# A new hand-written order and another layout of the attention weights in a one-core hash-attention and feed-forward kernel

## The chip, the core and the metric

One core of a Trainium2 chip runs the kernel. The core has TensorE (PE, the matrix unit), VectorE (DVE), ScalarE (ACT), GpSimd (POOL), SyncE (SP, which here only issues transfers) and 16 DMA engines. Every engine takes its own instructions strictly in the order in which they were written; semaphores tie the engines together. Matrix products land in PSUM, an accumulator memory of eight banks of 512 float32 for each of 128 partitions; everything else lives in SBUF.

The metric is the device time of one execution in microseconds (us); a median of several runs is given. The profile comes from one execution.

## The reference

Four batches, eight heads, 768 positions, head size 64; the model width is 512 and the hidden width 2048. Six sign bits of a projection give each query and key a bucket, and only keys of the query's own bucket are attended to. What follows is a layer norm, a two-layer feed-forward with a ReLU, and a residual.

```
q_bits = (einsum('bhsd,dk->bhsk', q, proj) > 0); k_bits likewise
q_bucket = sum(q_bits * powers); k_bucket likewise
mask = q_bucket[:, :, :, None] == k_bucket[:, :, None, :]
scores = where(mask, (q @ k.T) / sqrt(D), -1e9)
attn = softmax(scores) ; x = (attn @ v) laid out as (B, S, 512)
xn = (x - mean) / sqrt(var + 1e-6) * g_ln
out = x + relu(xn @ w_ch1) @ w_ch2
```

## The kernel before

The work is cut into twelve *units*: unit u is batch u // 3 and 256 of its 768 queries. A unit has six *steps*: two groups of four heads (g) times three blocks of 256 keys. Step s belongs to unit s // 6, so steps 0 to 17 are batch 0 and steps 18 to 71 are batches 1 to 3.

The kernel has no loops over this work. The string `ORDER` (lines 17 to 115) lists some 1,120 words such as `S.t.19.2`: an operation, the engine it is issued on (t TensorE, v VectorE, a ScalarE, p GpSimd, s SyncE) and its arguments. The last lines of the kernel body walk through the string and call one short function for each word. So the order of the words is the program order of every engine, of SP's and POOL's transfers too. The words that matter:

- `lx`, `tn`, `ca`, `ha`, `bi` (batch 0) and `LX`, `tu`, `CA`, `hm`, `bt`, `mo` (later batches): load queries and keys, transpose them (DVE, line 247), cast them to bf16, form the bucket bits (a small float32 product, then a comparison). `mo` is a DMA of 4.5 KB that puts one piece of the bits into place; there are 16 for each batch and group, 96 in all, on SP (line 421).
- `S` (line 444): 24 matmuls that make the scores of one step, 128 keys by 256 queries, twice, for four heads. The bucket bits enter as a further product, so that keys of another bucket come out far below zero.
- `E` (line 454): `exp` on ScalarE, PSUM to SBUF, 128 x 1024 elements, two instructions for each step (heads 0 and 1, heads 2 and 3): 144 in all.
- `A` (line 463): 16 matmuls for each step that multiply the exponentials with the values and a column of ones, into the two PSUM banks `acc`.
- `na`, `nb`, `nc`, `ce` (lines 474 to 489): DVE divides by the sum and makes the layer norm's statistics; `fl` (line 498) transposes the normalised rows by DMA, issued on SP.
- `F` (line 516): 8 matmuls for 256 of the hidden columns; `R` (line 524 on ScalarE, line 526 on VectorE): ReLU. Eight pairs for each unit, through one PSUM bank, `f1`.
- `D` (line 532): the second feed-forward product, 16 matmuls of 512 columns for each half of a unit, written as four quarters, into the bank `f2`. `Z` (line 541) adds the residual and `O` (line 545 on) stores.

PSUM is full: `scA` and `scB` (two banks each) for scores, `acc` (two), `f1` and `f2`. Before `acc` is first needed, the steps 0 to 5 rotate over three pairs, by the table `SC_PAIRS` at line 151.

The transposes work on 32 x 32 blocks, so a column of the scores stands for a query in a permuted order. Units 0 to 2 keep that order: the attention result comes out with permuted rows, and a unit is stored by four DMAs of 32 partitions and 128 KB each (`out_view`). From unit 3 on (`U_TURNED = 3`, line 163) `E` writes its output turned, each element four places from the one before it, so that rows come out in the order of the output tensor, and a unit is stored by one DMA of 128 partitions and 512 KB (`out_turned`, line 555). The last unit is stored in six pieces of 64 partitions (line 558).

Of the kernel before, what the change touches and what calls it, by code (L numbers as in the profile page):

```python
# [17 lines left out]
mem.v on.p.1 on.p.0 lp.a pf.v lx.s.0.1.1.3 tn.v.0.1.2 ca.p.0.1.2 tn.v.0.1.1 lx.s.0.0.0.1 tn.v.0.0.0 ca.a.0.0.0  # L18
ca.a.0.1.1 lx.s.1.0.0.1 warm.t ha.t.0.1.2 bi.v.0.1.2 tn.v.1.0.0 ca.p.1.0.0 ha.t.0.0.0 bi.v.0.0.0 lx.s.0.1.0.1
tn.v.0.1.0 ca.a.0.1.0 ha.t.1.0.0 bi.v.1.0.0 pmem.p p32.p S.t.2.2 E.a.2.1 E.a.2.0 lv.s.0.0.4 cv.p.0.0.2 ha.t.0.1.1  # L20
bi.v.0.1.1 ha.t.0.1.0 lx.s.1.1.0.3 tn.v.1.1.2 ca.p.1.1.2 S.t.1.2 E.a.1.1 E.a.1.0 lx.s.1.0.1.3 ha.t.1.1.2 bi.v.0.1.0
S.t.0.2 E.a.0.0 E.a.0.1 lg.s tn.v.1.1.1 ha.t.1.1.1 ca.p.1.1.1 bi.v.1.1.2 S.t.5.2 E.a.5.1 tn.v.1.1.0 ca.p.1.1.0
ha.t.1.1.0 cv.p.0.0.0 A.t.1.2 A.t.0.2 bi.v.1.1.1 lw1.p.0 E.a.5.0 S.t.4.2 E.a.4.1 lw1.p.1 lx.s.0.0.1.3 tn.v.0.0.2
tn.v.0.0.1 ha.t.0.0.1 ca.v.0.0.1 lw2.p.1 E.a.4.0 bi.v.1.1.0 sv.t.0 LX.s.1.0.1 tu.v.1.0.1.3 tu.v.1.0.1.1 tu.v.1.0.1.2
lw1.p.3 tu.v.1.0.1.0 lw2.p.0 CA.p.1.0.1.1 tn.v.1.0.2 A.t.2.2 bi.v.0.0.1 S.t.6.2 E.a.6.0 E.a.6.1 ha.t.1.0.2 sw.v.0
na.v.0.0 nb.v.0.0 S.t.3.2 nc.v.0.0 E.a.3.1 bi.v.1.0.2 ha.t.0.0.2 lv.s.0.4.4 cv.p.0.4.0 cv.p.0.4.2 sv.t.4 LX.s.1.0.0
tu.v.1.0.0.0 tu.v.1.0.0.2 lv.s.1.4.1 S.t.8.2 E.a.3.0 A.t.3.2 E.a.8.0 A.t.5.2 E.a.8.1 A.t.4.2 ca.v.1.0.2 tn.v.1.0.1
ca.v.1.0.1 bi.v.0.0.2 ha.t.1.0.1 S.t.7.2 E.a.7.1 E.a.7.0 LX.s.1.1.1 lw1.p.2 sw.v.4 na.v.0.1 nb.v.0.1 A.t.8.2
nc.v.0.1 A.t.6.2 ce.v.0.0 bi.v.1.0.1 ft.t.0.0 fc.a.0.0 S.t.10.2 E.a.10.0 E.a.10.1 ce.v.0.1 ft.t.0.1 rs.p.0
tu.v.1.0.0.1 A.t.7.2 fc.v.0.1 F.t.0.0 R.a.0.0 CA.v.1.0.0.0 LX.s.1.1.0 S.t.11.2 E.a.11.1 E.a.11.0 lw2.p.2  # L30
tu.v.1.0.0.3 CA.a.1.0.0.1 hm.t.1.0 bt.v.1.0 mo.s.1.0.3.0 mo.s.1.0.0.0 mo.s.1.0.2.3 mo.s.1.0.0.3 mo.s.1.0.1.2
mo.s.1.0.0.1 mo.s.1.0.1.3 mo.s.1.0.3.3 mo.s.1.0.0.2 F.t.0.7 R.v.0.7 lw2.p.3 S.t.9.2 E.a.9.1 CA.p.1.0.1.0 F.t.0.6
F.t.0.3 na.v.1.0 nb.v.1.0 A.t.10.2 ca.v.0.0.2 E.a.9.0 S.t.14.2 E.a.14.1 tu.v.1.1.0.3 A.t.9.2 R.v.0.6 mo.s.1.0.2.2
E.a.14.0 nc.v.1.0 R.v.0.3 lv.s.1.0.0 A.t.11.2 na.v.1.1 F.t.0.4 R.a.0.4 LX.s.2.1.1 F.t.0.1 R.a.0.1 S.t.13.2 E.a.13.0
E.a.13.1 nb.v.1.1 A.t.14.2 nc.v.1.1 ce.v.1.0 ce.v.1.1 fl.s.1.1 fl.s.1.0 F.t.0.5 R.a.0.5 tu.v.1.1.0.0 lv.s.1.4.2
F.t.0.2 R.a.0.2 LX.s.2.0.0 lv.s.1.4.3 lv.s.1.0.3 tu.v.1.1.0.1 mo.s.1.0.1.1 mo.s.1.0.1.0 mo.s.1.0.2.1 tu.v.1.1.1.3
S.t.12.2 E.a.12.1 E.a.12.0 tu.v.1.1.1.0 tu.v.1.1.0.2 CA.a.1.1.0.1 mo.s.1.0.2.0 lv.s.1.0.1 mo.s.1.0.3.1 LX.s.2.0.1
D.t.0.0.0 D.t.0.0.1 D.t.0.0.2 D.t.0.0.3 S.t.16.2 E.a.16.0 E.a.16.1 mo.s.1.0.3.2 tu.v.1.1.1.1 F.t.1.7 R.v.1.7
A.t.13.2 A.t.12.2 na.v.2.0 F.t.1.2 R.a.1.2 S.t.17.2 E.a.17.1 E.a.17.0 tu.v.1.1.1.2 CA.p.1.1.1.1 hm.t.1.1 Z.v.0.0
D.t.0.1.0 bt.v.1.1 mo.s.1.1.3.2 mo.s.1.1.3.0 mo.s.1.1.2.1 mo.s.1.1.1.1 mo.s.1.1.0.1 mo.s.1.1.0.0 mo.s.1.1.1.2  # L40
mo.s.1.1.3.1 F.t.1.0 R.a.1.0 S.t.15.2 E.a.15.0 E.a.15.1 rs.p.1 nb.v.2.0 nc.v.2.0 A.t.16.2 A.t.17.2 mo.s.1.1.0.3
CA.v.1.1.0.0 tu.v.2.0.1.2 tu.v.2.0.1.1 LX.s.2.1.0 F.t.1.6 R.a.1.6 D.t.0.1.1 CA.p.1.1.1.0 tu.v.2.0.0.0 mo.s.1.1.1.0
mo.s.1.1.0.2 lv.s.1.0.2 cv.p.1.0.0 A.t.15.2 na.v.2.1 nb.v.2.1 nc.v.2.1 ce.v.2.0 fl.s.2.0 ce.v.2.1 rs.p.2 on.p.2
F.t.1.5 R.a.1.5 S.t.19.2 E.a.19.0 F.t.1.3 R.a.1.3 tu.v.2.0.1.3 CA.p.2.0.1.1 mo.s.1.1.3.3 mo.s.1.1.1.3 E.a.19.1
fl.s.2.1 D.t.0.1.2 D.t.0.1.3 Z.v.0.1 O.s.0.3 tu.v.2.0.0.1 F.t.1.1 R.a.1.1 sa.p.1.0.1 S.t.20.2 tu.v.2.0.0.3
mo.s.1.1.2.0 tu.v.2.0.0.2 CA.v.2.0.0.1 tu.v.2.0.1.0 E.a.20.1 F.t.1.4 R.a.1.4 lv.s.1.4.0 cv.p.1.4.0 D.t.1.0.0
D.t.1.0.1 D.t.1.0.2 D.t.1.0.3 Z.v.1.0 E.a.20.0 S.t.18.2 E.a.18.0 mo.s.1.1.2.2 E.a.18.1 F.t.2.2 R.v.2.2 D.t.1.1.0
F.t.2.4 R.a.2.4 mo.s.1.1.2.3 S.t.22.2 E.a.22.0 F.t.2.1 R.v.2.1 cv.p.1.0.2 A.t.18.2 A.t.19.2 sa.p.1.0.0 sb.p.1.0
sa.p.1.0.2 lv.s.3.4.0 lv.s.3.4.2 lv.s.3.4.1 F.t.2.0 R.v.2.0 E.a.22.1 S.t.21.2 E.a.21.1 lv.s.3.4.3 su.p.1.0
sa.p.1.4.2 sa.p.1.4.1 sa.p.1.4.0 sb.p.1.4 E.a.21.0 A.t.20.2 sp.t.1.0 sc.v.1.0 na.v.3.0 nb.v.3.0 nc.v.3.0 D.t.1.1.1  # L50
F.t.2.5 R.v.2.5 S.t.23.2 E.a.23.0 E.a.23.1 D.t.1.1.2 D.t.1.1.3 O.s.0.0 F.t.2.7 CA.a.2.0.1.0 S.t.24.2 E.a.24.1
E.a.24.0 su.p.1.4 cv.p.1.4.2 lv.s.2.0.3 lv.s.2.0.1 lv.s.2.0.2 A.t.22.2 R.v.2.7 sp.t.1.4 Z.v.1.1 O.s.1.3 O.s.1.2
O.s.1.0 A.t.23.2 A.t.21.2 sc.v.1.4 F.t.2.3 R.a.2.3 S.t.25.2 E.a.25.1 E.a.25.0 D.t.2.0.0 na.v.3.1 nb.v.3.1 nc.v.3.1
ce.v.3.0 fl.s.3.0 O.s.0.1 ce.v.3.1 rs.p.3 fl.s.3.1 CA.a.2.0.0.0 O.s.0.2 hm.t.2.0 tu.v.2.1.1.0 bt.v.2.0 mo.s.2.0.3.2
mo.s.2.0.3.1 mo.s.2.0.2.2 mo.s.2.0.1.0 mo.s.2.0.1.2 mo.s.2.0.0.0 tu.v.2.1.0.3 tu.v.2.1.1.2 mo.s.2.0.2.3 LX.s.3.0.0
S.t.26.2 E.a.26.0 E.a.26.1 mo.s.2.0.2.0 LX.s.3.1.0 tu.v.2.1.0.2 CA.v.2.1.0.1 mo.s.2.0.1.1 mo.s.2.0.0.2 D.t.2.0.1
D.t.2.0.2 F.t.2.6 R.a.2.6 tu.v.2.1.1.3 lv.s.2.0.0 mo.s.2.0.3.0 mo.s.2.0.2.1 S.t.28.2 E.a.28.1 E.a.28.0 A.t.26.2
F.t.3.7 R.v.3.7 A.t.24.2 D.t.2.0.3 Z.v.2.0 mo.s.2.0.1.3 S.t.29.2 E.a.29.0 E.a.29.1 O.s.1.1 mo.s.2.0.0.3 A.t.25.2
na.v.4.0 D.t.2.1.0 tu.v.2.1.1.1 LX.s.3.0.1 F.t.3.1 R.a.3.1 S.t.27.2 E.a.27.0 E.a.27.1 D.t.2.1.1 D.t.2.1.2
mo.s.2.0.3.3 sa.p.2.0.0 F.t.3.4 R.a.3.4 S.t.31.2 E.a.31.1 E.a.31.0 tu.v.2.1.0.1 F.t.3.0 R.a.3.0 nb.v.4.0 A.t.29.2  # L60
A.t.27.2 A.t.28.2 na.v.4.1 S.t.32.2 E.a.32.0 E.a.32.1 F.t.3.5 R.v.3.5 CA.p.2.1.1.1 CA.p.2.1.1.0 D.t.2.1.3 Z.v.2.1
O.s.2.2 F.t.3.3 R.a.3.3 S.t.30.2 E.a.30.1 F.t.3.2 R.a.3.2 nc.v.4.0 D.t.3.0.0 E.a.30.0 nb.v.4.1 A.t.32.2 F.t.3.6
nc.v.4.1 ce.v.4.1 fl.s.4.1 R.a.3.6 ce.v.4.0 fl.s.4.0 S.t.34.2 E.a.34.1 E.a.34.0 A.t.30.2 O.s.2.0 mo.s.2.0.0.1
cv.p.2.0.2 tu.v.2.1.0.0 CA.v.2.1.0.0 LX.s.3.1.1 D.t.3.0.1 hm.t.2.1 tu.v.3.0.0.2 bt.v.2.1 mo.s.2.1.3.2 mo.s.2.1.0.1
mo.s.2.1.1.0 tu.v.3.0.0.1 mo.s.2.1.3.0 mo.s.2.1.3.1 mo.s.2.1.0.0 mo.s.2.1.0.2 mo.s.2.1.2.1 mo.s.2.1.1.3 mo.s.2.1.2.2
tu.v.3.0.1.1 mo.s.2.1.1.1 cv.p.2.0.0 S.t.33.2 E.a.33.0 E.a.33.1 A.t.31.2 sa.p.2.0.2 mo.s.2.1.0.3 tu.v.3.0.1.3
F.t.4.5 R.a.4.5 tu.v.3.0.1.0 tu.v.3.0.0.3 CA.a.3.0.0.1 D.t.3.0.2 D.t.3.0.3 Z.v.3.0 F.t.4.3 R.a.4.3 CA.p.3.0.1.0
rs.p.4 tu.v.3.0.0.0 S.t.35.2 E.a.35.1 E.a.35.0 mo.s.2.1.1.2 F.t.4.6 R.v.4.6 D.t.3.1.0 O.s.2.1 CA.a.3.0.0.0
sa.p.2.0.1 sb.p.2.0 lv.s.2.4.2 lv.s.2.4.3 su.p.2.0 lv.s.2.4.1 lv.s.2.4.0 F.t.4.0 R.a.4.0 S.t.37.2 E.a.37.0 E.a.37.1
na.v.5.0 nb.v.5.0 A.t.35.2 A.t.34.2 nc.v.5.0 O.s.2.3 mo.s.2.1.2.0 F.t.4.2 R.a.4.2 tu.v.3.0.1.2 CA.a.3.0.1.1 A.t.33.2  # L70
na.v.5.1 nb.v.5.1 nc.v.5.1 ce.v.5.1 fl.s.5.1 cv.p.3.4.2 ce.v.5.0 fl.s.5.0 S.t.36.2 E.a.36.1 E.a.36.0 F.t.4.1 R.a.4.1
cv.p.2.4.0 D.t.3.1.1 D.t.3.1.2 D.t.3.1.3 Z.v.3.1 O.s.3.2 sa.p.2.4.2 mo.s.2.1.2.3 A.t.36.2 F.t.4.7 R.a.4.7 S.t.38.2
E.a.38.1 F.t.4.4 R.v.4.4 D.t.4.0.0 D.t.4.0.1 E.a.38.0 S.t.42.2 F.t.5.4 R.v.5.4 D.t.4.0.2 D.t.4.0.3 Z.v.4.0
sa.p.2.4.1 F.t.5.3 R.v.5.3 mo.s.2.1.3.3 A.t.38.2 on.p.3 E.a.42.0 sa.p.2.4.0 E.a.42.1 S.t.39.2 E.a.39.1 E.a.39.0
sp.t.2.0 sc.v.2.0 D.t.4.1.0 A.t.37.2 na.v.6.0 nb.v.6.0 nc.v.6.0 F.t.5.6 R.a.5.6 S.t.41.2 E.a.41.0 E.a.41.1 D.t.4.1.1
D.t.4.1.2 D.t.4.1.3 Z.v.4.1 O.s.4.1 F.t.5.2 R.a.5.2 S.t.40.2 E.a.40.0 F.t.5.0 R.v.5.0 cv.p.2.4.2 A.t.41.2 lv.s.3.0.1
A.t.39.2 lv.s.3.0.2 F.t.5.1 sb.p.2.4 su.p.2.4 E.a.40.1 S.t.44.2 E.a.44.1 E.a.44.0 lv.s.3.0.0 A.t.40.2 lv.s.3.0.3
# [40 lines left out]
def kernel(  # L118
# [122 lines left out]
    def E(s):  # L241
        return sb(f"E{s}", [P, 4, 512], BF16, "E", 4)
# [206 lines left out]
    def E_(eng, s, h):  # L449
        dst, src = E(s)[:, heads(h)], sc(s, h)  # L450
        if s // 6 >= U_TURNED:
            dst = dst.rearrange("p i (n t c) -> p (i n) c t", t=TT, c=CC)
            src = src.rearrange("p i (n c t) -> p (i n) c t", t=TT, c=CC)
# [148 lines left out]
```

## Time and profile before

| | us |
|---|---|
| median of 3 runs | 427.36 |
| lowest, highest | 426.16, 427.93 |
| the profiled execution's own time | 426.16 |
| its span, first to last instruction | 424.5 |

The span's busy times, of 424.5 us: PE 325.6, weight loads (PEld, beside PE) 221.1, DVE 169.9, ACT 336.3, POOL 72.5. 33.58 MB move by DMA, 80 GB/s from and to memory over the span.

| stretch, us | what runs | PE busy | ACT busy | granted TensorE clock |
|---|---|---|---|---|
| 0 to 20 | loads, first bits, first steps | 18.0 | 12.3 | 1.00 |
| 20 to 39.8 | first units, first F | 18.4 | 15.9 | 1.00 |
| 39.8 to 67.7 | steps 9 to 19, batch 1's preparation | 27.5 | 20.5 | 1.00 |
| 67.7 to 393.5 | steps 18 to 71 with F and D between | 234.7 of 325.8 | 282.2 | 0.92 |
| 393.5 to 418.9 | F and D of the last units | 25.2 | 5.4 | 1.00 |

How to read it: an engine that is busy for a whole stretch sets the stretch's length unless a wait hides in it. The profile models the end of pipelined matmuls, so a matmul's "mean ns" is longer than the time it takes from the next; the time that a block of matmuls costs is read from start to start in the timeline. "Idle before" is the time an engine waited before a group, with what ended the wait. The granted clock is the share of full speed that the TensorE clock had.

### The profile page before, as it was taken

How to read it: one execution, taken by the hardware profiler on the slowest of the kernel's cores; microseconds unless marked ns; L12 is line 12 of the kernel's file. 1: busy time of each engine (PE TensorE's matmuls, PEld its weight loads, DVE VectorE, ACT ScalarE, POOL GpSimd, SP SyncE). 2: the span in 40 equal slices, each digit the busy share in tenths (PEclk: the TensorE clock that was granted, in tenths of full speed). 3: DMA queues.
4: the chain of work that ended last, by engine and by line, in shares of the span. 5: the costliest groups of instructions: out<-in, count | busy, mean ns of one | idle time of the engine just before them, and what ended most of it. 6: DMA issues, size and time to landing. Idle time of an engine off the chain costs nothing.

```text
span 424.5 us, 9805 instructions
## 1 busy us (share of the span) xinstructions
PE 325.6 (77%) x4319; PEld 221.1 (52%) x4360; DVE 169.9 (40%) x348; ACT 336.3 (79%) x215; POOL 72.5 (17%) x112
## 2 busy tenths in 40 slices
PE   8999998786567765687786667966787666887996
PEld 6677765464444544554454445544445344545664
DVE  5786848132522154432233616143116025214521
ACT  4878867988989888988888898879889989868121
POOL 3823020640104003150002302501001000100100
PEclk9999999988998899988898989899899989868999
DMA  8999894251253031420041001101101100200212
GB/s 265 363 277 207 178 245 116 48 144 39 52 163 98 2 85 45 102 76 2 2 124 26 6 3 23 61 2 25 52 2 55 21 2 2 76 2 0 76 42 59
DMA packets 29947, 33.58 MB, mean 79 GB/s; under 512 B 15057, under 2 KB 26577, under 8 KB 29905
## 3 DMA queue, kind: packets, MB, share of 16 engines
q1 hardware_dynamic: 25360, 28.50, 23.0%
q0 software_dynamic: 4224, 4.19, 6.0%
q8 instruction: 34, 0.56, 0.5%
q10 hardware_dynamic: 320, 0.26, 0.3%
q14 instruction: 9, 0.07, 0.0%
HBM read 27.53 MB, written 6.29 MB: 80 GB/s over the span
## 4 chain that ended last, share of the span: by engine, by line
ACT 55%; PE 29%; issue 5%; SPq 4%; DMA 3%; DVE 2%; ACTq 0%; DVEq 0%
ACT E L454 54%; PE sc L444 13%; PE f L516 6%; DMA X<-in_q_dram 3%; SPq L421 2%; PE acc L463 1%; PE f_41None L532 1%; DMA xnT<-xc 1%; SPq L295 1%; PE f_90None L532 1%; PE f_100None L532 1%; PE f_101None L532 1%; PE f L532 1%; PE f_110None L532 1%; PE f_91None L532 1%
## 5 line engine op out<-in xcount | busy, mean ns | idle before, releaser
L454 ACT ACTIVATE E<-sc,bias_sb 128x1024 bf16<-128x1024 f32 x144 | 299.8, 2184 | 48.7 <-PE sc L444 47.6
L516 PE MATMUL f<-xnT,w_sb 128*128 128x256 bf16 x768 | 107.7, 288 | 7.1 <-ACT hb L524 5.6
L444 PE MATMUL sc<-G 6*128 6x256 bf16 x576 | 51.2, 282 | 77.7 <-ACT E L454 77.0
L516 PEld LDWEIGHTS <-w_sb 128*128 128x128 bf16 x768 | 74.5, 102 | 35.4 <-issue 18.1
L444 PEld LDWEIGHTS <-G 6*128 6x128 bf16 x576 | 22.6, 93 | 98.9 <-issue 93.9
L526 DVE TENSOR_SCALAR hb<-f 128x512 bf16<-128x512 f32 x39 | 26.9, 689 | 106.4 <-PE f L516 106.3
L532 PEld LDWEIGHTS <-hb 128*128 128x128 bf16 x400 | 40.7, 105 | 43.2 <-issue 15.7
L444 PE MATMUL sc<-qb,kb 32*128 32x256 bf16 x1152 | 59.3, 282 | 0.0
L524 ACT ACTIVATE hb<-f 128x512 bf16<-128x512 f32 x57 | 36.7, 646 | 25.2 <-PE f L516 25.1
L463 PE MATMUL acc<-vaug,E 128*128 128x65 bf16 x1152 | 46.0, 198 | 3.5 <-ACT E L454 3.4
L463 PEld LDWEIGHTS <-E 128*128 128x128 bf16 x1152 | 42.4, 101 | 11.1 <-ACT E L454 5.0
L494 POOL TENSOR_SCALAR rs<-mv 128x2 f32<-128x2 f32 x12 | 7.1, 594 | 179.3 <-DVE mv L488 179.0
L444 PEld LDWEIGHTS <-kb 32*128 32x128 bf16 x1152 | 35.0, 97 | 1.1
L247 DVE STREAM_TRANSPOSE T<-X 128x384 f32<-128x384 f32 x48 | 24.8, 553 | 14.0 <-PE hp L409 10.3
L474 DVE SCALAR_TENSOR_TENSOR acc<-vsB,acc 128x520 f32<-128x520 f32 x24 | 16.8, 702 | 29.3 <-PE acc L463 29.0
L357 POOL TENSOR_TENSOR t<-vn 128x256 f32<-128x256 f32 x18 | 13.2, 744 | 51.9 <-DMA vn<-in_v_dram 34.3
L489 DVE SCALAR_TENSOR_TENSOR xc<-x,mv,gB 128x512 bf16<-128x512 f32 x24 | 18.3, 764 | 0.9
L485 DVE BATCH_NORM_STATS2 st<-x 128x6 f32<-128x256 f32 x48 | 18.0, 417 | 0.7
L347 POOL CAST vaug<-vn 128x768 bf16<-128x768 f32 x16 | 13.5, 861 | 28.0 <-DMA vn<-in_v_dram 16.3
L258 POOL CAST kb<-T 128x768 bf16<-128x768 f32 x10 | 8.4, 847 | 57.4 <-DVE T L247 57.4
L481 DVE TENSOR_TENSOR x<-acc,rc 128x512 f32<-128x512 f32 x24 | 16.6, 691 | 0.8
L316 PE MATMUL hf<-tp,pfull 128*128 128x256 f32 x48 | 13.2, 401 | 0.8 <-DVE tp L247 0.8
(98 smaller groups left out, 233.1 us busy)
## 6 DMA issues: line engine op xcount, KB each, us to landing
X<-in_k_dram SPq DMA_DIRECT2D x7, 768.0 KB
X<-in_q_dram SPq DMA_DIRECT2D x6, 768.0 KB
vn<-in_v_dram SPq DMA_DIRECT2D x24, 192.0 KB
w_sb<-in_moe_w_ch_dram POOLq DMA_DIRECT2D x8, 512.0 KB, 16.4
out_dram<-x SPq DMA_DIRECT2D x8, 512.0 KB
out_dram<-x SPq DMA_DIRECT2D x13, 128.0 KB
vn<-in_v_dram SPq DMA_DIRECT2D x2, 768.0 KB
G<-B SPq DMA_DIRECT2D x96, 4.5 KB
```

What stands on the lines that cost most here:

```text
L247: nc.vector.transpose(d[:, j], s[:, j, kj0 : kj0 + n])
L444: nc.tensor.matmul(sc(s, i // 2)[:, i % 2, 256 * kk : 256 * kk + 256], lh, rh, start=(rep == 0), stop=(rep == 2), skip_group_check=True,)
L454: nc.scalar.activation(dst, src, AF.Exp, scale=EXP_SCALE, bias=bias_sb)
L463: nc.tensor.matmul(acc[:, qt, (D + 1) * i : (D + 1) * (i + 1)], E(s)[:, i, 256 * kk + P * qt : 256 * kk + P * qt + P], vaug(u // 3)[:, 4 * ...
L474: nc.vector.scalar_tensor_tensor(acc, vs, EPS_ROW, acc, op0=AOP.mult, op1=AOP.add)
L481: nc.vector.tensor_tensor(xo, a[:, :, :, 0:D], rc.to_broadcast([P, 2, 4, D]), op=AOP.mult)
L485: nc.vector.bn_stats(stats(u)[:, qt, g], xt(u)[:, qt, 256 * g : 256 * g + 256])
L489: nc.vector.scalar_tensor_tensor(xc(u)[:, t], xt(u)[:, t], mv(u)[:, t, 0:1], gB, op0=AOP.subtract, op1=AOP.mult,)
L516: nc.tensor.matmul(f1[:, n].rearrange("p (t x) -> p t x", t=2), w1_sb[:, dt, P * nt : P * nt + P], xnT(u)[:, :, dt], start=(dt == 0), stop ...
L524: nc.scalar.activation(hb(u)[:, 2 * p : 2 * p + 2], f1, AF.Relu)
L526: eng.tensor_scalar_max(hb(u)[:, 2 * p : 2 * p + 2], f1, 0.0)
L532: nc.tensor.matmul(f2, hb(u)[:, nt, P * t : P * t + P], w2_sb[:, nt, half(h)], start=(nt == 0), stop=(nt == NNT - 1),)
```

## The change

Five things change; the arithmetic stays the same.

1. `E` writes its output in the order in which it reads, in all units. `U_TURNED`, `out_turned` and the two rearranged views are gone.
2. `O` stores every unit by 32 partitions: four DMAs of 128 KB, where units 3 to 10 had one of 512 KB. The last unit is stored in twelve pieces instead of six. The ORDER has 56 `O` words instead of 26, 49 of them on SP (before 23) and 7 on ScalarE's queue (before 3).
3. `SC_PAIRS` has three steps (0, 1, 2) instead of six; from step 3 on every step uses `scA` and `scB`.
4. Steps 3 and 4 are issued in halves of two heads (`S.t.3.0`, `S.t.3.1` and so on), in `S` and in `A`.
5. `ORDER` is another string throughout. Its multiset of words is the same apart from the above and the choice of engine for a few: 52 ReLUs on ScalarE and 44 on VectorE instead of 57 and 39; the casts `CA` 4 on ScalarE, 12 on GpSimd and 8 on VectorE instead of 7, 10 and 7; four casts and copies of the first units moved likewise. The start differs most: the load of `g_ln` (`lg`) now stands before all loads of queries and keys, step 0 comes first with loads of one third of its group's queries and keys only. The first steps run 0, 1, 2, 3, 4, 5, 8; before, they ran 2, 1, 0, 5, 4, 6, 3.

```
-SC_PAIRS = {2: ("scA","scB"), 0: ("acc","scA"), 1: ("scB","acc"), 4: ("scA","scB"), 3: ("acc","scA"), 5: ("scB","acc")}
+SC_PAIRS = {0: ("scA", "scB"), 1: ("acc", "scA"), 2: ("scB", "acc")}
-U_TURNED = 3
-out_turned = [out[b].rearrange("(p u qt) d -> u p qt d", u=3, qt=2) for b in range(B)]
 def E_(eng, s, h):
-    dst, src = E(s)[:, heads(h)], sc(s, h)
-    if s // 6 >= U_TURNED:
-        dst = dst.rearrange("p i (n t c) -> p (i n) c t", t=TT, c=CC)
-        src = src.rearrange("p i (n c t) -> p (i n) c t", t=TT, c=CC)
-    nc.scalar.activation(dst, src, AF.Exp, scale=EXP_SCALE, bias=bias_sb)
+    nc.scalar.activation(E(s)[:, heads(h)], sc(s, h), AF.Exp, scale=EXP_SCALE, bias=bias_sb)
 def O_(eng, u, *a):
...
-    if u < U_TURNED:
-        eng.dma_start(out=out_view[u // 3][u % 3][c][:, t, half(h)], in_=xt(u)[32 * c : 32 * c + 32, t, half(h)])
-    elif u < NU - 1:
-        eng.dma_start(out=out_turned[u // 3][u % 3], in_=xt(u))
-    else:
-        r = slice(64 * c, 64 * c + 64)
-        eng.dma_start(out=out_turned[u // 3][u % 3][r, t, half(h)], in_=xt(u)[r, t, half(h)])
+    eng.dma_start(out=out_view[u // 3][u % 3][c][:, t, half(h)], in_=xt(u)[32 * c : 32 * c + 32, t, half(h)])
```

The head of `ORDER`, cut:

```
-mem.v on.p.1 on.p.0 lp.a pf.v lx.s.0.1.1.3 tn.v.0.1.2 ca.p.0.1.2 tn.v.0.1.1 lx.s.0.0.0.1 tn.v.0.0.0 ...
-... S.t.2.2 E.a.2.1 E.a.2.0 ... S.t.1.2 ... S.t.0.2 ... lg.s ... S.t.5.2 ... S.t.4.2 ... S.t.6.2 ... S.t.3.2
+mem.v pmem.p lg.s lp.a warm.t lx.s.0.0.0.1 tn.v.0.0.0 ca.a.0.0.0 pf.v ha.t.0.0.0 lx.s.0.1.0.1 tn.v.0.1.0 ...
+... S.t.0.2 E.a.0.0 E.a.0.1 ... S.t.1.2 ... S.t.2.2 ... S.t.3.0 E.a.3.0 S.t.3.1 E.a.3.1 ... S.t.4.0 ... S.t.5.2
```

Its end, the stores of the last half unit:

```
-D.t.11.1.3.0 Z.v.11.1.0 O.s.11.1.0.0 O.a.11.1.1.0
+D.t.11.1.3.0 Z.v.11.1.0 O.s.11.1.0.0 O.s.11.1.1.0 O.a.11.1.2.0 O.a.11.1.3.0
```

## The prediction

> **What bounds the kernel now.** I read the page's busy times first, then the chain of waits, then ScalarE's groups in two stretches, then TensorE's timeline where it was densest. The page's busy rows and its chain:
>
> ```profile
> PE 325.6 (77%) x4319; PEld 221.1 (52%) x4360; DVE 169.9 (40%) x348; ACT 336.3 (79%) x215; POOL 72.5 (17%) x112
> ...
> ACT 55%; PE 29%; issue 5%; SPq 4%; DMA 3%; DVE 2%; ACTq 0%; DVEq 0%
> ```
>
> Two engines are near 80% and neither is full, but the chain that ended last goes through ScalarE for 55% of the span, nearly all of it the exponentials. The shares are averages over two regimes, so the next view is ScalarE's groups, first from 28 to 67 us (steps of batch 0), then from 67.8 to 388 us. Columns: instructions and shapes, count, busy us, mean ns, idle us before.
>
> ```profile
> L454 ACT ACTIVATE E<-sc,bias_sb 128x1024 bf16<-128x1024 f32 x22 | 23.3, 1110 | 6.4 <-PE sc L444 5.3 <-PE acc L463 1.0
> ```
>
> ```profile
> L454 ACT ACTIVATE E<-sc,bias_sb 128x1024 bf16<-128x1024 f32 x106 | 257.0, 2542 | 38.7 <-PE sc L444 38.7
> ```
>
> The same instruction on the same shape takes 1.110 us in batch 0 and 2.542 us afterwards. The only thing in the code that differs between the two is the turned write. The chain in order of time shows what that does (start us, duration us, what):
>
> ```profile
> 104.29 4.83 ACT E L454 x2
> 109.12 0.04 issue
> 109.16 0.89 PE sc L444 x24
> ...
> 110.14 4.85 ACT E L454 x2
> ...
> 121.70 4.83 ACT E L454 x2
> ```
>
> A step is 4.83 us of two exponentials, then 0.89 us of scores for which TensorE had to wait: `scA` and `scB` are both taken until `E` has read them. The pitch over three steps is (121.70 - 104.29) / 3 = 5.80 us. The dense stretch of batch 0 shows TensorE without that wait:
>
> ```profile
> 42.36 0.65 PE L463 MATMUL acc<-vaug,E 128*128 128x65 bf16 x16
> 42.95 0.29 PE L444 MATMUL sc<-G 6*128 6x256 bf16 x4
> ...
> 43.72 1.15 PE L463 MATMUL acc<-vaug,E 128*128 128x65 bf16 x32
> 44.71 1.91 PE L516 MATMUL f<-xnT,w_sb 128*128 128x256 bf16 x16
> ...
> 50.44 3.63 PE L532 MATMUL f_00None<-w_sb,hb 128*128 128x512 bf16 x15
> 54.00 0.29 PE L444 MATMUL sc<-G 6*128 6x256 bf16 x4
> ```
>
> From start to start: `S` 43.72 - 42.95 = 0.77 us, `A` (44.71 - 43.72) / 2 = 0.50 a step, `D` 54.00 - 50.44 = 3.56 for 16 matmuls (one record is missing), 0.89 a quarter. `F` is 0.88 (two from 40.60 to 42.36), `hm` 1.44 (37.41 to 38.85), `ha` about 1.0, the sum over values 0.77. The granted clock there was 1.00.
>
> **The change part by part, and the sum.** The sum is made against the profiled execution: 426.16 us, of which 424.5 are span and 1.7 lie around it. The runs shown have a median of 427.36, 1.2 above it.
>
> *Turned write removed.* 108 exponentials (steps 18 to 71) go from 2.542 to 1.110 us each by those rows. In pairs it is 4.83 against 2.12 (the pair at 62.87 us), because two overlap a little: 54 x 2.71 = 146 us leave ScalarE, whose busy time drops from 336 to about 190. This is the path, but TensorE's work takes over long before 146 us are gained. The Trainium skill ("ScalarE: Activation LUTs", "What ACT_TABLE_LOAD costs") speaks against a gain: every activation runs one element per cycle and lane, about 280 ns + 0.833 ns an element with a bias pointer, an estimate of 1.13 us here whatever the order of writing. The unturned row agrees; the turned row, 2.542, doesn't. By that rule the sum would be a gain of nothing.
>
> *TensorE's sum.* The work is the same in both kernels: 72 x 0.77 + 72 x 0.50 + 96 x 0.88 + 96 x 0.89 + 6 x 1.44 + 12 x 1.0 and 3.2 of small products = 285 us. With the first product at 5.6 us and 3.8 us from the last matmul (420.67) to the end it can't go under 294 us. The new order places the work thus, priced by these rows: 60.3 us before step 18, the 21st step issued, 193.4 us from there to the last step's scores, 31.5 us from there to the end.
>
> *Start.* The old order had 56.9 us of such work before step 19's scores, the first turned ones, at 66.95 us, so 10.1 us were start and idling. I give the new start the same: step 18 at 60.3 + 10.1 = 70.4 us. The load of `g_ln` (0.61 us of SP, 256 KB) now stands ahead of the first queries; step 0 needs 512 KB more, step 2 needed 1 MB before its scores at 9.03. The first two loads moved about 265 GB/s on the page, so 256 KB is about 1 us against a smaller need: between 2 us lost and 3 us gained, taken as nothing.
>
> *Middle.* The price of a step is the larger of its TensorE work and the exponentials' loop, now 2.12 + 0.89 + 0.1 = 3.1 us. The plan's TensorE work between scores is 3.0 to 5.8 us, and the sum of the larger one over the 52 steps is 193.7 us. The same formula on the old order with 5.80 instead of 3.1 gives 307.4 where the trace has 319.5 (66.95 to 386.45), 4% more. I take those 4%: 201.5 us. If no ReLU or cast on ScalarE (0.60 to 0.87 us each) overlapped with scores, the sum would be 202, the same. The bounds are 193.7, and 228 at the efficiency of the start (0.85, first rival).
>
> *Tail.* 31.5 by prices; the old one took 34.2 (386.45 to 420.67), its first part with turned exponentials. I take 33, then 3.8.
>
> *More stores.* 26 more issues on SP at 0.43 us (its row) are 11 us over the run, hidden: SP then holds 96 x 0.77 + 22 x 1.25 + 49 x 0.43 + about 22 for the loads, 145 us of a span of 309. Four more on ScalarE's queue, 0.5 each, have its idle time as cover. Exposed are only the last two queues' second pieces: +0.5. If the cover is gone, a unit's store delays the transposes `fl` queued behind it on SP, hence the next `F`; that is the first rival. The Trainium skill ("SBUF — State Buffer", "Door 1: The DMA port swizzle") says that 32 partitions reach half of the DMA ports; no run here shows it, and by its 189 GB/s against 328 a unit's four pieces are an estimated 2.8 us of transfer instead of 1.6, which nothing but the last unit waits for, so the sum would grow by an estimated 0.3 us.
>
> *Halves, bank rotation, engines.* Steps 3 and 4 keep their 24 and 16 matmuls; a half may start when one pair of banks is free. It costs at most an issue gap of 0.21 us for each of the four halves, bounds -1 to +1, taken as nothing. Five ReLUs from ScalarE (0.65) to DVE (0.69): DVE is at 170 us and has room.
>
> Sum: 70.4 + 201.5 + 33 + 3.8 + 0.5 = 309.2 us of span, + 1.7 = **311 us**.
>
> **The rivals.**
> 1. *A wait other than the exponentials takes over* (18 in 100). From 39.57 to 79 us SP issued almost without a gap, mostly `mo` at 0.77 us, and the chain ran through SP and the transposed load xnT (4.15 us) there. SP's 145 us are a third of the old span and nearly half of the new one, and more than that while `mo` words are issued, so `fl` or the bits could come late. The old stretch up to 39.8 us did 29.2 us of priced work in the 34.2 us after 5.6, 0.85. At that rate the 225 us of work from step 18 on take 265: 70.4 + 265 + 4.3 + 1.7 = 341. Against it: the stretch from 39.8 to 67.7 did 27.1 us of work in 27.9 with SP as busy as that. Partly true, it gives 322 to 341.
> 2. *The new start wins more* (5 in 100): TensorE packed from 5.6 us on, 294 + 5 of gaps in the middle (0.8 us in each 27.9, as from 39.8 to 67.7, over 194 us) + 1.7 = 301.
> 3. *The change doesn't do what it says; slower* (2 in 100). If the exponentials were long because of what runs beside them after 67 us (matmuls into the neighbouring banks), not because of the write, they would stay at 2.542. ScalarE's loop stays 5.80 us a step, nothing is gained, and the twelve last pieces and 26 issues add 2 us: 429. It decides if the mean of line 454 after 70 us is above 2.4. Against: `E` is 2.12 a pair at 62.87 us and 2.55 each from 67.82, with TensorE equally full on both sides; steps 17 and 19 differ by the write alone.
>
> **How the numbers follow.** The forecast, 303 to 321 us, has 75 in 100. The predicted time is its middle. The range of 8 in 10 takes in the unknown bounds: 302 (the middle at its lower bound, 8 us less, and a start 1 us earlier) to 332 (half of the first rival). About 0.5% is what a measurement can tell here. Faster by more than that is everything but the last rival: 0.975; within it 0.005; slower 0.02.
>
> **What would show it.** Line 454: 144 at about 1.11 us, 153 us busy. ScalarE about 190 busy. TensorE above 90% of the span, granted clock near 1.00 throughout instead of 0.92 after 67.7 us (the clock fell only where TensorE waited). A step's pitch of 3.1 to 4 us instead of 5.80. The chain led by PE, not by line 454. The prediction is wrong if line 454 stays above 2 us, if TensorE idles for more than 10% after 70 us, or if its granted clock falls below 0.95 while it is full: 5% of 225 us is 11 us.

## The result and the profile after

The changed kernel takes 311.5 us (median of four runs, 308.99 to 312.62) against 427.64 for the kernel before beside it: a ratio of 0.727, with a 95% interval of 0.721 to 0.733. The forecast was 311. Its profiled execution took 311.38 us with a span of 309.7.

The busy rows, the granted clock over 40 slices and the chain by engine, from the page of the changed kernel:

```profile
PE 296.0 (96%) x4317; PEld 207.6 (67%) x4360; DVE 171.4 (55%) x351; ACT 190.1 (61%) x208; POOL 77.0 (25%) x116
...
PEclk9999999999899999999999999999999999999999
...
PE 84%; DMA 6%; DVE 5%; ACT 2%; issue 1%; SPq 1%; ACTq 0%
```

ScalarE's 336 us have become 190, and TensorE is busy for 96% of a span that is 115 us shorter. TensorE's own busy time fell too, from 325.6 to 296.0 us, though it does the same products: its clock hardly drops any more (a mean of 0.994 over the whole run, 0.935 before). The chain that ended last now goes through TensorE, where ScalarE had 55% of it.

ScalarE's groups from 67.8 to 280 us, the stretch in which the exponentials took 2.542 us each:

```profile
L450 ACT ACTIVATE E<-sc,bias_sb 128x1024 bf16<-128x1024 f32 x109 | 116.4, 1111 | 46.2 <-PE sc L444 46.2
```

`E` waited for scores before too (38.7 us). What has changed is the other direction: TensorE's waits for an exponential ahead of scores, first in the kernel before, then in the changed one (us in all, times, longest):

```profile
PE sc L444 <- ACT E L454: 77.0, 47, 2.6
```

```profile
PE sc L444 <- ACT E L450: 0.6, 1, 0.6
```

The chain of waits around 245 us shows the new pitch (start us, duration us, what):

```profile
245.06 0.87 PE f L512 x8
245.93 0.77 PE sc L444 x23
246.70 0.60 PE acc L459 x16
247.30 0.87 PE f L512 x8
248.23 0.81 PE f_80None L528 x3
249.04 0.77 PE sc L444 x24
```

From scores to scores it is 249.04 - 245.93 = 3.11 us, and TensorE goes from one product to the next with no wait for an exponential in it.

One larger wait is left. TensorE's timeline around 80 us, and its busy time in two stretches:

```profile
78.98 0.39 PE L444 MATMUL sc<-qb,kb 32*128 32x256 bf16 x8
81.29 1.14 PE L512 MATMUL f<-xnT,w_sb 128*128 128x256 bf16 x8 [1.93 <-DMA xnT<-xc]
```

```profile
80.00:85.00 5.00, 3.49 (x14) 1.87 (x16) 0.69 (x1) 1.52 (x2) 3.85 (x8) 0.71 0.38 60
85.00:90.00 5.00, 4.95 (x77) 3.67 (x77) 1.44 (x2) 2.62 (x3) 0.00 (x0) 0.95 0.95 272
```

Columns of the stretches: us, length, busy time (and records) of PE, PEld, DVE, ACT and POOL, then the granted clock, the DMA share and GB/s. The first `F` of unit 2 waits 1.93 us for its transposed rows, and the mean granted clock from 80 to 85 us is 0.71. Within that stretch it is 0.50 for 3.4 us:

```profile
82.12:85.52 3.40, 3.18 (x10) 1.27 (x9) 0.69 (x1) 0.00 (x0) 1.81 (x5) 0.50 0.24 57
```

### The profile page after: what moved, and what is told of

It is laid out like the page before. It is cut to its first block, busy times and chain, and to the rows that moved or that the text cites. A ratio compares the mean times of both kernels' runs of the same rounds, so it can differ in the third digit from the quotient of the medians.

```text
span 309.7 us, 9840 instructions
## 1 busy us (share of the span) xinstructions
PE 296.0 (96%) x4317; PEld 207.6 (67%) x4360; DVE 171.4 (55%) x351; ACT 190.1 (61%) x208; POOL 77.0 (25%) x116
## 4 chain that ended last, share of the span: by engine, by line
PE 84%; DMA 6%; DVE 5%; ACT 2%; issue 1%; SPq 1%; ACTq 0%
PE f L512 26%; PE sc L444 16%; PE acc L459 10%; PE hf L316 4%; DMA X<-in_q_dram 3%; PE hp L409 2%; DMA vn<-in_v_dram 2%; ACT E L450 1%; DMA xnT<-xc 1%; PE f L528 1%; PE f_71None L528 1%; PE f_90None L528 1%; PE f_81None L528 1%; PE f_21None L528 1%; PE f_101None L528 1%
## 5 line engine op out<-in xcount | busy, mean ns | idle before, releaser
L450 ACT ACTIVATE E<-sc,bias_sb 128x1024 bf16<-128x1024 f32 x144 | 153.4, 1111 | 57.9 <-PE sc L444 57.8
L512 PE MATMUL f<-xnT,w_sb 128*128 128x256 bf16 x768 | 99.6, 273 | 2.6 <-DMA xnT<-xc 1.9
L512 PEld LDWEIGHTS <-w_sb 128*128 128x128 bf16 x768 | 71.1, 98 | 26.6 <-issue 9.0
L522 DVE TENSOR_SCALAR hb<-f 128x512 bf16<-128x512 f32 x44 | 30.4, 691 | 59.3 <-PE f L512 59.0
L528 PEld LDWEIGHTS <-hb 128*128 128x128 bf16 x400 | 37.6, 99 | 34.1 <-issue 4.5
L520 ACT ACTIVATE hb<-f 128x512 bf16<-128x512 f32 x52 | 31.0, 596 | 46.0 <-PE f L512 45.7
L444 PE MATMUL sc<-qb,kb 32*128 32x256 bf16 x1152 | 53.0, 267 | 0.0
L444 PE MATMUL sc<-G 6*128 6x256 bf16 x576 | 41.8, 273 | 1.3 <-ACT E L450 0.6
L444 PEld LDWEIGHTS <-kb 32*128 32x128 bf16 x1152 | 30.7, 93 | 1.6
L444 PEld LDWEIGHTS <-G 6*128 6x128 bf16 x576 | 15.3, 91 | 19.1 <-issue 16.1
```

The costliest lines, as they stand in the source:

```text
L444: nc.tensor.matmul(sc(s, i // 2)[:, i % 2, 256 * kk : 256 * kk + 256], lh, rh, start=(rep == 0), stop=(rep == 2), skip_group_check=True,)
L450: nc.scalar.activation(E(s)[:, heads(h)], sc(s, h), AF.Exp, scale=EXP_SCALE, bias=bias_sb)
L512: nc.tensor.matmul(f1[:, n].rearrange("p (t x) -> p t x", t=2), w1_sb[:, dt, P * nt : P * nt + P], xnT(u)[:, :, dt], start=(dt == 0), stop ...
L520: nc.scalar.activation(hb(u)[:, 2 * p : 2 * p + 2], f1, AF.Relu)
L522: eng.tensor_scalar_max(hb(u)[:, 2 * p : 2 * p + 2], f1, 0.0)
L528: nc.tensor.matmul(f2, hb(u)[:, nt, P * t : P * t + P], w2_sb[:, nt, half(h)], start=(nt == 0), stop=(nt == NNT - 1),)
```

## The experiments

Ratios are to the kernel before, run beside each. Where several experiments were measured beside the same runs of the kernel before, this is said.

**The write alone, in the old order** (e1).

```
 # the kernel before, ORDER untouched
-    if s // 6 >= U_TURNED: (the turned views)
+    nc.scalar.activation(E(s)[:, heads(h)], sc(s, h), AF.Exp, scale=EXP_SCALE, bias=bias_sb)
 # stores: each O word of units 3 to 10 issues four DMAs of 32 partitions, each of unit 11 two
```

> The old order with the plain write of E in all units and the four stores a unit that go with it, nothing else changed. My theory (the turned write is the whole gain, the order little): 54 pairs lose 2.71 us each until TensorE binds; the larger of TensorE's work and 3.1 us over the old order's steps is 197 us, plus 4%, which gives 309 to 318 us; line of E at 1.11 us. Rival (the new order is what keeps TensorE full, the old one was planned for something else): the old order idles as its start does, 325 to 345 us. Rival (E is long for what runs beside it): 2.54 us a piece after step 18 and 427 to 430 us.

It took 305.26 us, ratio 0.716 (0.712 to 0.719). That is under the range that I had given for my theory. From its page:

```profile
PE 292.3 (96%) x4319; PEld 205.1 (68%) x4360; DVE 169.5 (56%) x348; ACT 194.5 (64%) x215; POOL 72.3 (24%) x112
```

The whole gain, and more than it, comes from the write. The new order does not add to it. (The stores changed here too; e7 below shows that they are level.)

**The new order alone, with the turned write** (e2, beside the same runs as e1).

```
 # the changed kernel
+    if s // 6 >= 3: (the turned views of the kernel before)
+    stores of units 3 to 11 go to rows 32c to 32c + 32 of the turned output view, four a unit
```

> The new order with the turned write of E from unit 3 on, and the four stores of a unit going to the turned rows. Theory: E at 2.54 us from step 18 on, pitch 5.8 us, the larger of TensorE's work and 5.8 us over 52 steps is 302 us plus 4%, with 70 before and 37 behind, + 1.7: 422 to 432 us. Rival (the order brings a part of the gain by itself): under 410 us.

430.22 us, ratio 1.009 (1.005 to 1.013): slower by about 1%. Its 144 exponentials take 300.4 us, as in the kernel before (299.8). The two edits are now apart: the write is worth 28% in the old order (e1), and with the turned write the new order, with its stores and bank rotation, costs 1%.

**Which property of the write costs** (e3; e8 below adds more forms). One kernel, run once, with four forms of the exponential's views, each on a line of its own.

```
+ units 3, 4:  dst "(n t c) -> n c t", src "(n c t) -> n c t", t=32, c=4   (as before the change)
+ units 5, 6:  dst "(n t c) -> n t c", src "(n c t) -> n t c", t=32, c=4   (same result, other loop order)
+ units 7, 8:  as units 3, 4 with t=64, c=2
+ units 9-11:  dst contiguous, src read in blocks of 32 elements, the blocks in another order
```

> The new order; E in units 3 and 4 writes turned as before the change (steps of 4 elements, 8 bytes), in units 5 and 6 it gives the same result but runs in the order of the output (contiguous write, PSUM read in steps of 32 elements), in units 7 and 8 it writes in steps of 2 elements (4 bytes, the queries of two halves interleaved), in units 9 to 11 in contiguous blocks of 32 elements in another block order. Output rows of units 3 to 11 are permuted, or mixed. Each form has a line of its own. Theory (the distance between neighbouring writes is what costs): 2.54, 1.11, between 1.11 and 2.54, and 1.11 us. Rival (more than one free dimension costs, whatever the steps): 2.54 in all four. Rival (any odd order costs, on the read side too): the second at 2 us or more, the last at 1.11.

ScalarE's groups of that kernel; lines 457, 461, 465 and 469 are the four forms in this order, 453 the plain one:

```profile
L457 ACT ACTIVATE E<-sc,bias_sb 128x1024 bf16<-128x1024 f32 x24 | 58.2, 2545 | 8.9 <-PE sc L444 8.9
L469 ACT ACTIVATE E<-sc,bias_sb 128x1024 bf16<-128x1024 f32 x36 | 38.4, 1112 | 16.3 <-PE sc L444 16.3
L453 ACT ACTIVATE E<-sc,bias_sb 128x1024 bf16<-128x1024 f32 x36 | 38.2, 1111 | 11.3 <-PE sc L444 11.2
L465 ACT ACTIVATE E<-sc,bias_sb 128x1024 bf16<-128x1024 f32 x24 | 32.3, 1403 | 12.2 <-PE sc L444 12.2
L461 ACT ACTIVATE E<-sc,bias_sb 128x1024 bf16<-128x1024 f32 x24 | 25.7, 1112 | 6.8 <-PE sc L444 6.8
```

Both rivals fall: the forms with more free dimensions do not all take 2.54 us, and reading PSUM in steps of 32 elements (461) or from block to block (469) takes 1.112 us, as the plain form does. (The expectation speaks of contiguous blocks in the last form; in its code the write is contiguous throughout, and only the read goes from block to block.) The step between neighbouring writes costs: 1.11 us contiguous, 1.40 at two elements, 2.545 at four. Line 461 computes what the kernel before computed, at the price of the plain write.

**The same edit as a kernel** (e7). The kernel before with the two loops of the turned views exchanged, and nothing else:

```
-            dst = dst.rearrange("p i (n t c) -> p (i n) c t", t=TT, c=CC)
-            src = src.rearrange("p i (n c t) -> p (i n) c t", t=TT, c=CC)
+            dst = dst.rearrange("p i (n t c) -> p (i n) t c", t=TT, c=CC)
+            src = src.rearrange("p i (n c t) -> p (i n) t c", t=TT, c=CC)
```

> The kernel before with one edit: E runs through its elements in the order of the output, so that it writes contiguously and reads PSUM in steps of 32 elements; the result, the single stores of units 3 to 10 and the order are those of before. Theory (the step between neighbouring writes was the whole cost; SP has room, so stores by one or by four DMAs are level): E at 1.11 us, time 303 to 307 us, within 1.5 us of the old order with the plain write. Rival (fewer, larger stores free SP or the DMA engines): 300 to 303. Rival (the read in steps costs TensorE, which writes the neighbouring banks): E at 1.11 but TensorE's rows longer, over 308.

304.58 us, ratio 0.7145 (0.7116 to 0.7174), level with e1: turned rows with one store a unit, or permuted rows with four, make no difference that these runs show. The group of `E` in it:

```profile
L454 ACT ACTIVATE E<-sc,bias_sb 128x1024 bf16<-128x1024 f32 x144 | 152.8, 1110 | 49.5 <-PE sc L444 48.4 <-PE acc L463 1.1
```

**Where the new order loses: the start** (e4; e4 to e7 were measured beside the same runs of the kernel before).

```
-mem.v pmem.p lg.s lp.a warm.t lx.s.0.0.0.1 tn.v.0.0.0 ca.a.0.0.0 pf.v ha.t.0.0.0
+mem.v pmem.p lp.a warm.t lx.s.0.0.0.1 pf.v tn.v.0.0.0 ca.a.0.0.0 ha.t.0.0.0
 ... lx.s.1.1.0.3 ... S.t.3.1 E.a.3.1
-lv.s.0.0.4
+lv.s.0.0.4 lg.s
```

> The changed kernel with two words of its start moved: the load of g_ln goes behind the loads of the first two groups' queries and keys, the copies of the projection go ahead of the first transposes. Theory (part of the 6.7 us of span that the new order costs against the old one, both with the plain write, is lost at the start: scores of the first step at 11.2 us against 9.1, step 18 3.3 us later by the work before it): first scores at about 9 us, span 1.5 to 3 us shorter, 307 to 310 us. Rival (the start's lead is eaten by the wait for the second group's data or at 81 us): first scores early, time within 1 us of the changed kernel, 310 to 312.

313.37 us, ratio 0.7325 (0.728 to 0.737): no gain. The lead is eaten, as the rival said, but at another wait, and the time is above the rival's 310 to 312. The first scores start at 8.16 us instead of 11.21 (9.65 in e5 and e11, whose start is that of the changed kernel), but the lead is gone by 27 us. VectorE's and TensorE's timelines there:

```profile
24.90 1.50 DVE L245 STREAM_TRANSPOSE T<-X 128x384 f32<-128x384 f32 x3 [2.74 <-DMA X<-in_q_dram]
```

```profile
26.76 0.86 PE L367 MATMUL vp<-vaug,ones 128*128 128x260 bf16 x6 [2.57 <-DVE G L248]
```

Transposes of batch 1's queries (`tu`) stand in VectorE's queue ahead of the comparison that frees the bank for the sum over values. The transposes start at 24.9 us here, in the changed kernel and in e5 and e11, whether the first scores are early or late, because they wait for the queries; so VectorE waits 2.74 us for them and TensorE 2.57 us for VectorE. The first `F` starts at 36.51 us; in the changed kernel it was 36.49.

**Where it loses: the wait at 81 us** (e5).

```
-... cv.p.1.0.2 tu.v.2.0.0.2 E.a.17.0 ... ce.v.2.1 fl.s.2.1
+... cv.p.1.0.2 E.a.17.0 ... ce.v.2.1 tu.v.2.0.0.2 fl.s.2.1 mo.s.1.1.2.3 mo.s.1.1.0.1
 (the two mo words stood before F.t.1.0)
```

> The changed kernel with three words moved around 70 us: the transposes tu 2.0.0.2 go behind the layer norm of unit 2's two halves, and two mo words go behind unit 2's transposed stores on SP. Theory (unit 2's first F waits 1.9 us for xnT, then TensorE runs at a granted clock of 0.71 from 80 to 85 us: 3.6 us in all, because xc was late behind a transposition that waited for queries, and fl behind mo): the wait goes below 0.5 us, the clock stays at 1.00, time 307 to 309 us. Rival (the late word is only replaced by the next late one, the queries' load or the bits of unit 3): the wait moves and the time stays at 310 to 312.

The wait for xnT is gone from TensorE's list and the granted clock stays at 1.00 from 80 to 90 us. The first scores of step 23 start at 83.64 us instead of 87.05, with the step before it at the same place (78.62, 78.52), and the profiled span is 307.1. But the rest of step 23's scores now wait 0.46 us for the bits of unit 3, as the rival said, and the runs do not follow: 310.84 us, ratio 0.729 (0.725 to 0.732), level with the changed kernel.

The clock is not the edit's doing. In e11 below the unaltered changed kernel was profiled again, and the same word waits 1.68 us with no fall of the clock behind it:

```profile
82.54 1.05 PE L512 MATMUL f<-xnT,w_sb 128*128 128x256 bf16 x8 [1.68 <-DMA xnT<-xc]
```

```profile
80.00:85.00 5.00, 3.32 (x41) 2.08 (x41) 0.69 (x1) 2.72 (x3) 4.76 (x7) 1.00 0.48 66
85.00:90.00 5.00, 5.00 (x82) 3.89 (x81) 1.44 (x2) 2.72 (x3) 0.50 (x3) 1.00 0.90 251
```

There the half clock comes at 36.8 us instead. From the scores of step 18 to those of the last step the changed kernel took 200.5 us in its first profile and 198.4 in e11; e5 took 197.9. So the edit removes the wait, but against e11 only 0.4 us of it is left by the last step; the other 2.2 us lie between two executions of one kernel, most of it the clock. The runs agree: with a mean granted clock of 1.000 the changed kernel took 308.49 and 308.99 us, e5 308.79 and 308.94.

**Both** (e6).

> Both edits together. Theory (two separate losses): the gains add, 304 to 307 us, level with the old order and the plain write (305.3). Rival (one loss hides the other): no better than the better one of the two alone.

312.05 us, ratio 0.732 (0.729 to 0.736): the gains do not add. TensorE's waits in that kernel:

```profile
PE vp L367 <- DVE G L248: 4.7, 1, 4.7
```

In this execution batch 1's queries were there only at 26.4 us, and the wait before the sum over values is longer than in e4 (2.57).

**The transposes out of VectorE's way** (e9; e6 plus one move).

```
-tu.v.1.0.0.2 tu.v.1.0.0.0 tu.v.1.0.0.1 lv.s.1.0.2 ... bi.v.0.0.1 ... nc.v.0.0
+lv.s.1.0.2 ... bi.v.0.0.1 ... nc.v.0.0 tu.v.1.0.0.2 tu.v.1.0.0.0 tu.v.1.0.0.1
```

> Start and stall edits together, and three transposes of batch 1's queries (tu 1.0.0.2, 0 and 1) go behind unit 0's first layer norm words on VectorE. Theory (the start's gain of 3 us was lost because these transposes stand first in VectorE's queue and wait for queries that land at 24.9 us whatever the start does; the bits and the copies that TensorE needs stand behind them): TensorE's wait of 4.7 us in front of the sum over values goes below 1 us, first F before 35 us, time 4 to 6 us under the kernel with start and stall edits: 306 to 308 us. Rival (the start is bound by the loads themselves, 1.2 of the DMA engines' share from 20 to 40 us): the wait moves on to the next word that needs a load, first F at 36 us or later, 310 to 313 us.

309.83 us, ratio 0.724 (0.720 to 0.727): some 2 us under e6, not the 306 to 308 of my theory, and level with e10, measured beside the same runs. The 4.7 us are gone and the first `F` is earlier, at 34.90 us instead of 36.49, as the theory had it; now it waits for another load, its weights, as the rival had it:

```profile
34.90 3.58 PE L510 MATMUL f<-xnT,w_sb 128*128 128x256 bf16 x16 [0.90 <-DMA w_sb<-in_moe_w_ch_dram]
```

Step 18 still starts at 73.94 us, as late as in the changed kernel (73.86). What ate this lead is the clock: these 16 matmuls take 3.58 us instead of 1.91, since the granted clock is 0.50 for 3.4 us from 34.95 us on. Neither side holds whole. At an equal clock e9 is ahead: its two runs with a mean granted clock of 0.994 took 308.03 and 308.61 us, where the changed kernel took 310.70 to 311.38, but in its other four the clock was lower. The DMA engines' share is above 1.1 from 20 to 36 us in the changed kernel, e4, e5, e6 and e9 alike.

**Halves or whole steps** (e10, beside the same runs as e9).

```
-S.t.3.0 E.a.3.0 S.t.3.1 E.a.3.1 ... S.t.4.0 E.a.4.0 S.t.4.1 E.a.4.1
+S.t.3.2 E.a.3.0 E.a.3.1 ... S.t.4.2 E.a.4.0 E.a.4.1
```

> The changed kernel with steps 3 and 4 issued whole in their scores instead of in halves, all else the same. Theory (halves are level): within 1 us of the changed kernel, 310 to 313. Rival (the halves let TensorE start 1 us earlier on a free pair of banks and matter at the start): 1 to 2 us slower, 313 to 315.

309.8 us, ratio 0.724 (0.720 to 0.727), level with the changed kernel. The products `A` of these steps stayed in halves.

**More forms of the write** (e8, run once).

```
+ units 3, 4:  dst "(n t c) -> n c t", src "(n c t) -> n c t", t=16, c=8
+ units 5, 6:  the same with t=4, c=32
+ units 7, 8:  pairs of neighbours, 32 elements from pair to pair
+ units 9-11:  dst contiguous, PSUM read in steps of 4 elements
```

> The new order; E in units 3 and 4 writes in steps of 8 elements (16 bytes), in units 5 and 6 in steps of 32 elements, in units 7 and 8 in pairs of neighbours with 32 elements between pairs, in units 9 to 11 contiguously while reading PSUM in steps of 4 elements. Output rows of units 3 to 11 are permuted or mixed. Theory (a lone bf16 write costs more the farther its neighbour is, up to a ceiling, and reading in steps is free): 2.5 us or more for the first two, 1.4 us or less for pairs (as for steps of 2), 1.11 us for the last. Rival (the cost grows with the step without a ceiling): 4 us and more for the first two. Rival (each separate 4-byte word costs the same, so pairs are as free as a contiguous write): 1.11 us for pairs.

Lines 457, 461, 465 and 469 in this order:

```profile
L457 ACT ACTIVATE E<-sc,bias_sb 128x1024 bf16<-128x1024 f32 x24 | 112.5, 4919 | 14.9 <-PE sc L444 14.9
L461 ACT ACTIVATE E<-sc,bias_sb 128x1024 bf16<-128x1024 f32 x24 | 110.7, 4817 | 15.6 <-PE sc L444 15.6
L469 ACT ACTIVATE E<-sc,bias_sb 128x1024 bf16<-128x1024 f32 x36 | 38.3, 1111 | 17.0 <-PE sc L444 17.0
...
L465 ACT ACTIVATE E<-sc,bias_sb 128x1024 bf16<-128x1024 f32 x24 | 26.0, 1129 | 13.7 <-PE sc L444 13.7
```

There is a ceiling, but twice as high as I had thought: 4.9 us at steps of 16 bytes and 4.8 at 64. Pairs of neighbours with 64 bytes from pair to pair are nearly free (1.13 us). That also answers a rival not named above, the length of the innermost loop: it shrinks with the growing step (64, 32, 16 and 4 elements), but the pairs have the shortest, two elements, and hardly cost.

**The two orders side by side** (e11 and e12, beside the same runs of the kernel before).

> The changed kernel unaltered, on the same chip and beside the same runs of the kernel before as the old order with the read turned, to compare the two orders directly. Theory (the new order is 2% slower than the old one once both write contiguously): 309 to 313 us. Rival (the difference came from different chips): within 1.5 us of the other.

> The old order with the read turned, unaltered, beside the changed kernel on the same chip. Theory: 303 to 307 us, 5 to 8 us under the changed kernel. Rival (different chips): within 1.5 us of it.

310.78 us, ratio 0.7246 (0.7221 to 0.7270), against 305.51, ratio 0.7146 (0.7120 to 0.7172). The intervals are apart: with a contiguous write in both, the old order is 5.3 us faster than the new one. A part of it is the clock: the mean granted clock was 0.998 or more in 15 of the 16 runs of the old order (e1, e7, e12), but in only 3 of the 10 of the changed kernel. Among these runs the medians are 305.06 and 308.99 us, 3.9 apart.

## Why the prediction was right

| term | predicted, us | measured, us |
|---|---|---|
| `E` after step 18 | 1.110 each | 1.111 each |
| ScalarE busy | about 190 | 190.1 |
| start: step 18's scores at | 70.4 | 73.86 |
| middle: to the last step's scores | 201.5 | 200.5 (73.86 to 274.38) |
| tail to the last matmul's end | 33 | 31.4 (to 305.8) |
| from there to the end | 4.3 | 3.9 |
| span | 309.2 | 309.7 |

*The mechanism was right and is shown from both sides.* e1 takes the turned write away and leaves the order, e2 does the opposite; the gain goes with the write. The rival that the exponentials are long for what runs beside them falls with e3, where the same kernel shows 2.545, 1.403 and 1.11 us for the same shape, and with e7, where exchanging two loops is the only edit.

*Pricing a step by the larger of TensorE's work and the exponentials' loop* gave 193.7 us, and the 4% on top, taken from the old order, brought it to 201.5, within 1 us of the measured 200.5. But the 4% stood in for something else here: of the 6.8 us above 193.7, 1.9 are the one wait at 81 us and an estimated 1.7 the 3.4 us at half the clock. In e11 the same stretch took 198.4 us. That the sum fits to 1 us is in part luck.

*The start is the term that I mis-sized.* I gave the new start the old one's 10.1 us of idling, "between 2 us lost and 3 us gained, taken as nothing". It idles 13.6 us: 3.5 us more than taken, and 1.5 outside the bound of 2 us lost. I had priced the load of `g_ln` against the smaller need of step 0, and not who stands behind whom: batch 1's queries and the first weights land when the loads allow, and the new order puts words that wait for them ahead of words that TensorE needs (e4 and e9 show the two waits; that they make up the 3.5 us is not shown). Shorter tail terms hid the error: +3.5, -1.0, -1.6 and -0.4 make +0.5. A forecast that is 0.5 us off had a 3.5 us error in it; so close a number is luck.

*Three slips do no harm.* Step 18 is the 20th step issued in the new order, not the 21st, and 60.3 us is the work ahead of the 20th. Step 19's scores start at 66.88 us in the trace, not 66.95. The middle of 303 to 321 is 312, not the predicted 311.

*The first rival came true at one place.* SP and the transposed rows did become a wait, for 1.93 us, not for the 10 to 30 us of that rival.

*Stores, halves and rotation.* More stores are hidden, as priced: e1 and e7 differ in them and are level, and the end after the last matmul took 3.9 us against 3.8 before. Scores in halves or whole are level (e10). The bank rotation by itself was not tried.

*What stays open.* The old order is 5.3 us faster. In the changed kernel's first profile 3.5 us of it lie before step 18 and most of the rest at 81 us, the wait and the half clock together. Undoing these places word by word gave 1 to 2 us at most in the medians, and the changed kernel's own two medians are 0.7 apart. Why the clock falls more often in the new order is not shown, and which order of loads would free its start was not tried. The fastest version that was run is the kernel before with two loops exchanged (e7, 304.58 and 305.51 us).

## What to carry to other kernels

When an instruction of one shape has two durations in one profile, find the access pattern that differs before touching the schedule; here exchanging two loops, so that the write is contiguous and the read takes the steps, was worth more than a new order of 1,150 words. Price a schedule's steady part by the larger of the bound engine's work and the loop that feeds it, step by step; with an allowance of 4% that was good to 1% here. Price its start by when loads land and by what stands behind each waiting word: in e4 an earlier first product only met the wait for the next load. And before a gain or a loss of 2 us is put down to an edit, compare the granted clocks of several executions.

## What the runs showed of the hardware

ScalarE's write of bf16 to SBUF, 128 x 1024 elements from PSUM:

| step between neighbouring writes | us |
|---|---|
| contiguous | 1.11 |
| pairs of neighbours, then 64 bytes | 1.13 |
| 4 bytes | 1.40 |
| 8 bytes | 2.54 |
| 16 bytes | 4.92 |
| 64 bytes | 4.82 |

Reading PSUM in steps of 4 or 32 float32, or in blocks of 32 in another order, with a contiguous write: 1.11. I had not expected the cost to double again at 16 bytes, nor a pair of neighbours to be nearly free with the next pair 64 bytes away.

The Trainium skill ("SBUF — State Buffer", "Door 1: The DMA port swizzle") calls a step of up to 8 bf16 elements free, since accesses within a 16-byte line run at full rate. These runs do not agree for ScalarE's writes: steps of 2 and 4 elements already cost 1.26 and 2.3 times the contiguous write.

The granted clock is low where TensorE waits often: 0.69 from 118 to 330 us in e8, where TensorE was busy for 120 of 212 us, and 0.92 from 67.7 to 393.5 us in the kernel before. With the waits for exponentials gone it was 0.994 over the run, and TensorE's busy time fell by 29.6 us (325.6 to 296.0).

Up to the last matmul, the traces of the kernels that write contiguously show it at 1.00 but for stretches at 0.50 of 3.4 us (once, in e6, of 6.8 us). TensorE can be full in such a stretch: in e12 from 11.1 to 14.5 us it was busy throughout. A single wait does not decide it: behind the wait at 81 us the half clock came in two traces (1.93 us each, the changed kernel and e4) and not in two others (1.68 us in e11, 1.17 in e10). In e11 it came at 36.8 us instead, behind waits of 1.15 and 0.61 us, which e5 has too (1.16 and 0.61) without it. One such stretch goes with some 2 us of time: the changed kernel took 308.49 and 308.99 us with a mean granted clock of 1.000, 310.70 to 311.38 at 0.994 (five runs), and 311.61 and 312.62 at 0.989.
